# Attention and two expert layers: first-batch products tile by tile on three rotating PSUM banks, and some row sums by squares on ScalarE

## The chip, the core and the metric

The kernel runs on one core of a Trainium2 chip. Its engines run side by side and wait for each other by semaphores: TensorE (PE, its weight loads counted as PEld), VectorE (DVE), ScalarE (ACT), GpSimd (POOL) and SyncE (SP), the last two mostly issuing DMA. The metric is the device time of one execution in microseconds.

## What is computed

Block-causal attention, a gated product layer, and a squared-ReLU layer:

```python
def reference(q, k, v, w1, w2, w3, w_out, w_in, w_out2):   # cut
    scores = q @ k.T / sqrt(64)                # B 4, H 8, S 576, D 64
    scores = where(block_i >= block_j, scores, -1e9)   # blocks of 64
    x = softmax(scores) @ v                    # as 2304 tokens x 512
    a, b = x @ w1, x @ w2                      # 512 -> 1024
    x = ((a * b) @ w3) @ w_out                 # 1024 -> 1024 -> 512
    g = relu(x @ w_in) ** 2                    # 512 -> 2048
    return g @ w_out2                          # 2048 -> 512
```

## The kernel before

The inputs come as raw 64-bit words. A weight tile is converted by two ACT and two DVE instructions (`convert`, L287: ACT L319 and L323, DVE L329 and L332) and then split into a high and a low piece, so that three products of pieces give one accurate product. A w1/w2 tile (`w12_tile(f)`, f from 0 to 7, L380) holds 128 columns of w1 and the same 128 of w2. It needs a scale first: the squared row sums of its two halves (`wsum`; half 0 by an ACT Square with an accumulator, L407, half 1 by a DVE reduction L394 and a tiny square L400) go through a two-column matmul (`norm_scale`, L351) and a few tiny DVE instructions, and then ACT (L278) writes the high piece and DVE (L281) the low one, half by half.

Attention runs in 16 pairs of heads, 4 pairs for each of the 4 batches. A pair has score matmuls (`s`, L757), row maxima on DVE (`nm`, L783 and L791), exponentials on ACT (L816), multiplications by the reciprocal sums (`p`, ACT L857, DVE L864), and the product with v into `pv_bank` (L949). ACT and DVE split that into the pieces of x for the products: `x0h`, `x0l` for token group 0 (320 tokens of the batch), `x1h`, `x1l` for group 1 (256 tokens); DVE's low piece is L965. Pairs 0 to 3 take another way, through transposes `tp` (L900).

`w3 @ w_out` is folded first, row block by row block (`setup_rows(i)`, i from 0 to 7, L1089: products `po`, evictions `w3o` on ACT L1116 and DVE L1121). For each batch `first_block(b, g)` then makes, for group 0 and after it for group 1, the products `ab` of x with all eight w1/w2 tiles (`accumulate`, 12 matmuls for w1 and 12 for w2, emitted in chunks of 6, at L1040), evicts them (`a`: ACT L1166, DVE L1184), splits their product into high and low (`g`: ACT L239, DVE L242) and multiplies by `w3o` (`y`, L1040). After the last batch's x come the normalisations and the second layer (`second_block`).

PSUM holds a pool of five banks for attention and, until all of rows, transposes and scales of the first batch are through, a pool with one `po` bank and two `tp` banks. `begin_blocks` (L1131) closes the latter and opens a pool of three `mm` banks for `ab` and `y`; it is a step that waits for every user of the old pool.

A planner (`Order.emit`, L117) writes each engine's list: an instruction has a key, a cost and the steps it needs, and the planner picks among the ready ones by key and by its own count of time. The key of the n-th conversion comes from `conv_key` (L1854); for the w1/w2 tiles it is

```python
K12 + K12S * (n - 13)      # K12 = 60, K12S = 2
```

`SPARE` is a planner's allowance for the attention steps of pairs 4 and later. Where the planner's own clock has a gap on PE early in the program, `warm_up(gap)` (L520) fills it with 128-wide dummy matmuls, one per 0.11 of the gap. `x_scale_0` (L433) takes the largest absolute v of the first batch's four pairs, by four DVE reductions of 640 elements (L440), for the scale of the first batch's x.

Of the kernel before, what the change touches and what calls it, by code (L numbers as in the profile page):

```python
# [7 lines left out]
F32 = mybir.dt.float32  # L8
# [11 lines left out]
P = 128  # L20
# [3 lines left out]
DM = H * D  # L24
# [146 lines left out]
def fused_kernel(ctx: ExitStack, tc: tile.TileContext, qT, kT, vp, va, w12, w3t, wo, wb, out):  # L171
# [32 lines left out]
    ps0_stack = ExitStack()  # L204
    pools["p0"] = ps0_stack.enter_context(tc.tile_pool(name="ps0", bufs=1, space=PSUM, side="right"))
# [14 lines left out]
    K12 = 60.0  # L220
    K12S = 2.0
# [6 lines left out]
    SPARE = 2.0  # L228
    S_SPARE = 0.7
# [24 lines left out]
    ON_V = (1,)  # L254

# [124 lines left out]
    def w12_tile(f, after):  # L380
# [5 lines left out]
        for half in range(2):  # L386
# [3 lines left out]
            if half in ON_V:  # L390
# [13 lines left out]
            junk = at_buf("junk", 1, [P, 512], BF16, f"junk_{f}_{half}")  # L404
# [3 lines left out]
                    junk(), x(), AF.Square, accum_out=sums()[:, half : half + 1]  # L408
# [23 lines left out]
    def x_scale_0():  # L432
# [3 lines left out]
        for p in range(KDM):  # L436
            v = raws[p][2]
            od.op(
                DVE, c_dve(640),
                lambda v=v, p=p: dve.tensor_reduce(  # L440
                    out=vq()[:, p : p + 1], in_=v().rearrange("p a b c -> p (a b c)"), op=ALU.max, axis=AX.X,
                    apply_absolute_value=True,
                ),
                [(v,)], [(vq, p)], key,
            )
        m = at_buf("vq2", 1, [P, 1], F32, "vq2")
        od.op(
            DVE, c_dve(8), lambda: dve.tensor_reduce(out=m(), in_=vq(), op=ALU.max, axis=AX.X),
            [(vq, p) for p in range(KDM)], [(m,)], key,
        )  # L450
        od.op(
            DVE, c_dve(8), lambda: dve.tensor_tensor(out=m(), in0=m(), in1=m(), op=ALU.mult), [], [(m,)], key
# [41 lines left out]
    def spare(p):  # L494

        return SPARE if p >= KDM else 0.0
# [22 lines left out]
    warm_out = buf("p0", "po", 1, [P, 512], F32, "warm_out")  # L519
# [363 lines left out]
    def transpose(p, g, a, pf, weights, key):  # L883
# [7 lines left out]
        for part, (todo, n) in enumerate(((mains, P), (lasts, 64))):  # L891
            tp = buf("p0", "tp", 2, [P, 512], F32, f"tp_{name}_{part}")
# [151 lines left out]

    class Acc:
# [43 lines left out]
    def setup_rows(i):  # L1089
# [865 lines left out]
```

## Time and profile before

| what | us |
| --- | --- |
| median of 3 runs | 883.93 |
| the runs | 882.22, 883.93, 889.14 |
| profiled execution, its own time | 883.62 |
| its span in the trace | 881.5 |

Between span and time lie 2.1 us that the trace doesn't show. Views of the trace are of this one execution: busy time is the time in which an engine ran something, idle time ahead of a group is put down to whoever released it, and the granted clock is TensorE's as a share of full speed.

### The profile page before, as it was taken

To read this page: it belongs to the slowest core of one execution; us is meant where nothing else is said; L and a number is where in the kernel's file an instruction comes from. 1 tells how busy PE (TensorE), PEld (TensorE's weight loads), DVE (VectorE), ACT (ScalarE), POOL (GpSimd) and SP (SyncE) were. 2 spreads that over 40 slices of the span, in tenths; PEclk is the share of its full clock that TensorE was granted. 3 is DMA by queue.
4 is the path that set the end of the run, shared out by engine and by line. 5 is a ranking of instruction groups with operands and counts; after the bars stand their busy time and mean duration, and the time that the engine had idled before them with its cause. 6 is when DMAs were issued, how large, how long until landed. Compare 5 with 4: busy or idle time off the path is not lost.

```text
span 881.5 us, 18383 instructions
## 1 busy us (share of the span) xinstructions
PE 850.7 (97%) x7143; PEld 643.7 (73%) x7147; DVE 632.6 (72%) x1470; ACT 571.7 (65%) x1304; POOL 107.9 (12%) x202
## 2 busy tenths in 40 slices
PE   7799988899999999999999999999999999999998
PEld 6477875588877888779979877666666666666664
DVE  5987979888778787763993788997853474375443
ACT  5987878677766676774895696664544464464343
POOL 5111112020121101002221111000010000000000
PEclk8999998899999999999999999999999999999999
DMA  8833348589998999883563342000020002001001
GB/s 312 321 123 104 122 147 231 125 149 185 183 196 158 184 167 177 155 136 111 195 204 119 105 143 73 1 25 1 2 97 1 1 29 67 1 1 48 1 1 48
DMA packets 104247, 98.06 MB, mean 111 GB/s; under 512 B 82976, under 2 KB 86816, under 8 KB 102752
## 3 DMA queue, kind: packets, MB, share of 16 engines
q0 software_dynamic: 17568, 69.09, 24.6%
q1 hardware_dynamic: 86592, 27.80, 18.9%
q8 instruction: 56, 0.92, 0.4%
q14 instruction: 31, 0.25, 0.1%
HBM read 60.69 MB, written 9.44 MB: 80 GB/s over the span
## 4 chain that ended last, share of the span: by engine, by line
PE 59%; DVE 3%; ACT 1%; issue 0%; DVEq 0%
PE o L1785 20%; PE p L1721 16%; PE ab L1040 11%; PE y L1040 7%; PE h L1636 2%; PE pv_bank L949 1%; PE s L757 1%; PE ny L1343 0%; DVE s L1663 0%; DVE nm L791 0%; DVE g L271 0%; DVE ob L1795 0%; DVE c L1742 0%; DVE p L864 0%; PE nq L1464 0%
## 5 line engine op out<-in xcount | busy, mean ns | idle before, releaser
L1785 PE MATMUL o<-wb,g 128*128 128x512 f16 x864 | 194.5, 379 | 0.1
L1040 PEld LDWEIGHTS <-w 128*128 128x128 f16 x1536 | 147.8, 99 | 51.8 <-ACT w L278 4.7
L1785 PEld LDWEIGHTS <-g 128*128 128x128 f16 x864 | 84.0, 98 | 92.4 <-issue 0.6
L1040 PE MATMUL ab<-x0h,w 128*128 128x320 f16 x512 | 112.8, 307 | 6.8 <-ACT w L278 3.1
L1040 PE MATMUL y<-g,w3o 128*128 128x320 f32 (+1 forms) x768 | 110.1, 299 | 0.5 <-DVE g L242 0.5
L816 ACT ACTIVATE pf<-s,nm 128x192 f32<-128x192 f32 (+4 forms) x160 | 82.9, 527 | 39.6 <-DVE nm L799 39.5
L1040 PEld LDWEIGHTS y<-g,w3o 128*128 128x128 f32 x768 | 103.6, 188 | 3.8 <-issue 1.9
L1609 ACT ACTIVATE c<-c,beta 128x512 f32<-128x512 f32 x64 | 45.4, 713 | 81.5 <-DVE c L1742 81.4
L1040 PE MATMUL ab<-x1h,w 128*128 128x256 f16 x512 | 87.9, 273 | 0.5 <-DVE a L1184 0.5
L1721 PEld LDWEIGHTS <-wb 128*128 128x128 f16 x768 | 75.2, 98 | 15.8 <-issue 0.2
L271 DVE TENSOR_TENSOR g<-c,g 128x512 f16<-128x512 f32 x64 | 43.7, 689 | 48.8 <-ACT g L269 48.8
L1040 PE MATMUL ab<-x0l,w 128*128 128x320 f16 x256 | 78.4, 306 | 0.0
L864 DVE SCALAR_TENSOR_TENSOR p<-pf,r,p 128x192 f16<-128x192 f32 (+2 forms) x120 | 62.6, 546 | 16.4 <-ACT p L857 15.7
L1040 PE MATMUL ab<-x1l,w 128*128 128x256 f16 x256 | 69.8, 272 | 0.0
L857 ACT ACTIVATE p<-pf,r 128x192 f16<-128x192 f32 (+2 forms) x120 | 60.8, 559 | 5.0 <-ACT pf L816 1.6
L1040 PE MATMUL po<-wo,w 128*128 128x256 f32 (+1 forms) x360 | 55.5, 303 | 8.6 <-DVE w3o L1121 4.8
L1721 PEld LDWEIGHTS <-st 128*128 128x128 f16 x576 | 56.4, 98 | 7.4
L1742 DVE TENSOR_TENSOR c<-p,x 128x512 f32<-128x512 f32 x32 | 22.1, 690 | 50.9 <-PE p L1721 40.2
L1040 PEld LDWEIGHTS po<-wo,w 128*128 128x128 f32 x360 | 47.1, 195 | 14.0 <-DVE w3o L1121 3.9
L757 PE MATMUL s<-kraw,qraw 64*128 64x288 f32 (+4 forms) x384 | 54.5, 409 | 1.2 <-ACT pf L816 1.2
L332 DVE CUSTOM_DVE_ANT_0 cx<-raw,cx 128x1024 uint16<-128x1024 uint16 (+1 forms) x61 | 47.6, 781 | 2.9 <-ACT raw L323 0.4
L319 ACT ACTIVATE raw<-raw 128x512 f32<-128x512 f32 (+1 forms) x61 | 46.4, 763 | 1.6 <-DMA raw<-in_w 1.4
(213 smaller groups left out, 1645.6 us busy)
## 6 DMA issues: line engine op xcount, KB each, us to landing
raw<-in_wb POOLq DMA_DIRECT2D x32, 512.0 KB, 4.9
raw<-in_w3t POOLq DMA_DIRECT2D x8, 1024.0 KB, 12.6
raw<-in_w POOLq DMA_DIRECT2D x16, 512.0 KB, 5.0
vraw<-in_vp POOLq DMA_DIRECT2D x16, 320.0 KB, 4.9
qraw<-in_qT POOLq DMA_DIRECT2D x16, 288.0 KB, 4.1
kraw<-in_kT POOLq DMA_DIRECT2D x32, 144.0 KB, 4.3
yraw<-ydram POOLq DMA_DIRECT2D x8, 512.0 KB, 4.7
vmix<-v SPq DMA_DIRECT2D x24, 160.0 KB, 4.4
```

Of the source, the lines that this page charges most:

```text
L271: DVE, c_dve(n), lambda: dve.tensor_tensor(out=lo(), in0=src(), in1=hi(), op=ALU.subtract), kh + ks, kl, key
L319: act.activation(up, up, AF.Prelu, scale=2.0**-112, alpha=2.0**32)
L332: dve.tensor_tensor(out=x(), in0=x(), in1=words()[1], op=ALU.add)
L757: pe.matmul(o[:, h] if t == 4 else o, q()[rows, q_start(t) : q_start(t) + 128], keys_()[rows, c], start=True, stop=True,)
L816: act.activation(o, view(a, t), AF.Exp, bias=nm()[:, k, a : a + 1], scale=SCALE, accum_out=ssum()[:, k, a : a + 1],)
L857: lambda o=o, nk=nk, a=a, k=k, w=weights, p16=p16, r=r: act.activation(p16()[:, o : o + nk], w(a, k), AF.Copy, scale=r()[:, k, a : a + 1]),
L864: lambda o=o, nk=nk, a=a, k=k, w=weights, p16=p16, r=r: dve.scalar_tensor_tensor(out=p16()[:, o + nk : o + 2 * nk], in0=w(a, k), scalar=r( ...
L1040: pe.matmul(acc(), l, r, start=k == 0, stop=k == len(mms) - 1)
L1609: lambda: act.activation(src(), src(), AF.Relu, scale=beta()[:, j, k : k + 1]),
L1721: pe.matmul(acc()[:, TH * half : TH * half + TH], lhs(a, kc), y[yn]()[:, kc], start=n == 0, stop=n == len(mms) - 1,)
L1742: DVE, c_dve(n), lambda: dve.tensor_tensor(out=o(), in0=x(), in1=y(), op=ALU.add), r, w, K_EVICT
L1785: pe.matmul(o(), g[gx]()[:, cols], wt(f)[:, a, 512:1024], start=(begin and n == 0), stop=(last and n == 2),)
```

## The change

The old `begin_blocks` and its second PSUM pool go. One pool of a `po` bank and two `tp` banks stays for the whole program, and `bank3` hands them out in turn to every accumulation that used `mm`. `first_block` is now called once for a batch: in batch 0 it walks over the w1/w2 tiles, and for each tile does group 0 and then group 1, with the `y` products of both groups after all tiles; in batches 1 to 3 the order of the code is as it was. The pieces `g` of group 1 in batch 0 get a place of their own, the tiles that held the first w_out (`w8_0`, `w8_1`). Rows 6 and 7 of the fold are listed after pair 3, 512 wide in a bank of their own each (24 matmuls instead of 48 of 256). The row sums of the second halves of w1/w2 tiles 5, 6 and 7 are ACT Squares, and so are the four reductions of `x_scale_0`, whose result is now a sum of squares where it was the square of the largest value. The w1/w2 conversions have keys from 50 in steps of 4, the allowance of pairs 4 to 7 is 1.0, and the dummy matmuls after the first gap are counted at 0.062 each: 114 of them become 175 (in stretches of 45, 32, 1, 35, 1 before and 45, 40, 16, 58, 16 after).

```diff
@@ PSUM pools, planner numbers @@
-    pools["p0"] = ps0_stack.enter_context(tc.tile_pool(name="ps0", bufs=1, space=PSUM, side="right"))
+    pools["pm"] = ctx.enter_context(tc.tile_pool(name="psM", bufs=1, space=PSUM, side="right"))
...
-    K12 = 60.0
-    K12S = 2.0
+    K12 = 50.0
+    K12S = 4.0
...
     SPARE = 2.0
+    PO_SPLIT = 6
+    SPARE_1 = 1.0
...
+    SQ_A = 5
@@ w12_tile @@
-            if half in ON_V:
+            if half in ON_V and f < SQ_A:
@@ x_scale_0 @@
             od.op(
-                DVE, c_dve(640),
-                lambda v=v, p=p: dve.tensor_reduce(
-                    out=vq()[:, p : p + 1], in_=v().rearrange("p a b c -> p (a b c)"), op=ALU.max, axis=AX.X,
-                    apply_absolute_value=True,
+                ACT, c_act(640, 0.14),
+                lambda v=v, p=p, junk=junk: act.activation(
+                    junk(), v().rearrange("p a b c -> p (a b c)"), AF.Square, accum_out=vq()[:, p : p + 1]
                 ),
...
-            DVE, c_dve(8), lambda: dve.tensor_reduce(out=m(), in_=vq(), op=ALU.max, axis=AX.X),
+            DVE, c_dve(8), lambda: dve.tensor_reduce(out=m(), in_=vq(), op=ALU.add, axis=AX.X),
@@ warm_up @@
-        for _ in range(int((0.8 * gap - 0.2) / 0.11)):
+        n = int((0.8 * gap - 0.2) / warm_cost[0])
+        if n > 0:
+            warm_cost[0] = 0.062
+        for _ in range(n):
@@ Acc and its banks @@
+    def bank3(name):
+
+        n_bank3[0] += 1
+        tag, n = ("po", 1) if n_bank3[0] % 3 == 0 else ("tp", 2)
+        return buf("pm", tag, n, [P, 512], F32, name)
...
-        def __init__(self, n, name, pool_="pm", tag="mm", bufs=3, full=512):
-            self.b = buf(pool_, tag, bufs, [P, full], F32, name)
+        def __init__(self, n, name, *home):
+            self.b = buf(*home, [P, 512], F32, name) if home else bank3(name)
@@ setup_rows @@
-        for half in range(2) if i else (None,):
+        for half in range(2) if 0 < i < PO_SPLIT else (None,):
...
+            if i < PO_SPLIT:
+                acc = Half(po_bank[0], cols, range(2) if half is None else (half,))
+            else:
+                acc = Acc(DM, f"po_{i}")
@@ first_block; ab_products holds the old loop's body for one f and one group @@
-    def begin_blocks():
-
-        begin = od.op("N", 0.0, open_blocks)
...
+    def first_block(b):
+        gs = [Products() for _ in GS]
+        if b:
+            for g in range(2):
+                for f in range(KFF):
+                    ab_products(b, g, f, gs[g])
+                y_products(b, g, gs[g])
+            return
+        for f in range(KFF):
+            for g in range(2):
+                ab_products(b, g, f, gs[g])
+        for g in range(2):
+            y_products(b, g, gs[g])
@@ g_at: where the pieces of the products of group 1, batch 0, lie @@
+            if b or not g:
+                gs.tiles.append(g_buf(f // 4, name))
+            else:
+                gs.tiles.append(buf("base", f"w8_{f // 4}", 1, [P, 8 * gn], F32R, name))
@@ the program @@
-        setup_rows(i)
+        if i < PO_SPLIT:
+            setup_rows(i)
...
+            for i in range(PO_SPLIT, KFF):
+                setup_rows(i)
...
-            begin_blocks()
...
-        for g in range(2):
-            first_block(b, g)
+        first_block(b)
```

PE's list where the first batch's products begin, before. A name `ab_0_1_0_0` is batch 0, group 1, tile 0, w1 (a last 1 is w2); what follows is a buffer's number.

```order
L1040 MATMUL ab_0_0_0_0_1625<-x0h0_0_468,w12_0_1224 128x320
...
L1040 MATMUL ab_0_0_0_1_1650<-x0h0_0_468,w12_0_1224 128x320
...
L1040 MATMUL ab_0_0_1_0_1674<-x0h0_0_468,w12_0_1224 128x320
...
L1040 MATMUL ab_0_0_7_1_2156<-x0h0_0_468,w12_3_1995 128x320
...
L1040 MATMUL y_0_0_0_2089<-g_0_0_0_1695,w3o_1_731 128x320 x6
...
L1040 MATMUL ab_0_1_0_0_2471<-x1h0_0_524,w12_0_1224 128x256
```

The same place after:

```order
L1044 MATMUL po_6_1475<-wo_0_314,w3_6_1272 128x512 x6
...
L1044 MATMUL po_7_1569<-wo_0_314,w3_7_1482 128x512 x6
...
L1044 MATMUL ab_0_0_0_0_1657<-x0h0_0_532,w12_0_1254 128x320
...
L1044 MATMUL ab_0_1_0_0_1703<-x1h0_0_588,w12_0_1254 128x256
...
L1044 MATMUL ab_0_1_0_1_1726<-x1h0_0_588,w12_0_1254 128x256
...
L1044 MATMUL ab_0_0_1_0_1747<-x0h0_0_532,w12_0_1254 128x320
```

All sixteen products of group 0 and its first `y` stood ahead of group 1's; now tile 0 serves both groups before tile 1 comes, with rows 6 and 7 just ahead.

DVE's list around the split of the last w1/w2 tile, `w12_3` from `cx_28` and `cx_29`, before. `a_0_0_6` is the eviction of tile 6, `p16_4_2` and `nm_5_0` are softmax steps of pairs 4 and 5, `wsc` is the tile's scale.

```order
L1184 SCALAR_TENSOR_TENSOR a_0_0_6_2041<-ab_0_0_6_1_2029,ab_back_0_1203,a_0_0_6_2041 128x320
L357 TENSOR_SCALAR nh_14_2070<-pv_bank_256 128x2
L259 TENSOR_SCALAR wsc_7_2072<-nh_14_2070 128x2
L259 TENSOR_SCALAR w12_back_1201<-nh_14_2070 128x2
L425 TENSOR_SCALAR ab_back_0_1203<-w12_back_1201,isx_0_270 128x2
L864 SCALAR_TENSOR_TENSOR p16_4_2_0_2054<-pf_4_2_0_2025,r_4_2_2050,p16_4_2_0_2054 128x576
L242 TENSOR_TENSOR g_0_0_4_1941<-a_0_0_6_2041,g_0_0_4_1941 128x320
L281 SCALAR_TENSOR_TENSOR w12_3_1995<-cx_28_1959,wsc_7_2072,w12_3_1995 128x512
L281 SCALAR_TENSOR_TENSOR w12_3_1995<-cx_29_2023,wsc_7_2072,w12_3_1995 128x512
L864 SCALAR_TENSOR_TENSOR p16_4_2_1_2062<-pf_4_2_1_2036,r_4_2_2050,p16_4_2_1_2062 128x576
L774 MEMSET s_5_0_2064 64x2x2x64
L791 TENSOR_REDUCE nm_5_0_2111<-s_5_0_2064 128x2 x2
```

After, from the eviction of group 1's tile 5 on:

```order
L1192 SCALAR_TENSOR_TENSOR a_0_1_5_2257<-ab_0_1_5_1_2250,ab_back_0_1242,a_0_1_5_2257 128x256
...
L243 TENSOR_TENSOR g_0_1_4_2203<-a_0_1_5_2257,g_0_1_4_2203 128x256
L868 SCALAR_TENSOR_TENSOR p16_5_1_0_2278<-pf_5_1_0_2227,r_5_1_2268,p16_5_1_0_2278 128x448
...
L787 TENSOR_REDUCE nm_5_2_2338<-s_5_2_0_2283 128x1
...
L969 SCALAR_TENSOR_TENSOR x0l0_1_2366<-pv_bank_289,vback_1_1845,x0h0_1_2350 128x320
...
L261 TENSOR_SCALAR wsc_7_2454<-nh_14_2388 128x2
...
L283 SCALAR_TENSOR_TENSOR w12_3_2177<-cx_28_2179,wsc_7_2454,w12_3_2177 128x512
L283 SCALAR_TENSOR_TENSOR w12_3_2177<-cx_29_2352,wsc_7_2454,w12_3_2177 128x512
```

Behind the split there were pair 4's last multiplication and pair 5's first maxima; now pair 5's multiplications and last maxima, six evictions of group 1 and pair 4's `x0l0_1` stand ahead of it.

PE's list where batch 1 begins, before. Pair 7 is the last whose x batch 1's products need: `x0h3_1`, `x0l3_1`, from `pv_bank` after `pt_7_0`.

```order
L949 MATMUL pv_bank_256<-pt_7_0_0_2981,v16_7_2765 64x256
...
L1040 MATMUL y_0_1_3_3289<-g_0_1_0_2552,w3o_1_731 128x256 x6
...
L757 MATMUL s_8_2_0_3351<-kraw_8_2649,qraw_8_2640 128x288
...
L1040 MATMUL y_0_1_3_3289<-g_0_1_4_2896,w3o_3_1472 128x256 x6
...
L1040 MATMUL ab_1_0_0_0_3379<-x0h0_1_2168,w12_0_1224 128x320
...
L949 MATMUL pv_bank_256<-pt_7_1_0_3119,v16_7_2765 64x128
...
L1040 MATMUL ab_1_0_0_0_3379<-x0h3_1_3338,w12_0_1224 128x320
...
L1040 MATMUL ab_1_0_0_0_3379<-x0l3_1_3349,w12_0_1224 128x320
```

After:

```order
L1044 MATMUL y_0_1_3_3278<-g_0_1_4_2203,w3o_3_1579 128x256 x6
...
L1044 MATMUL ab_1_0_0_0_3320<-x0h0_1_2350,w12_0_1254 128x320
...
L1044 MATMUL ab_1_0_0_1_3331<-x0h0_1_2350,w12_0_1254 128x320
...
L761 MATMUL s_8_2_0_3340<-kraw_8_2748,qraw_8_2742 128x288
...
L953 MATMUL pv_bank_289<-pt_7_0_0_3052,v16_7_2844 64x256
...
L1044 MATMUL ab_1_0_0_0_3320<-x0h2_1_3055,w12_0_1254 128x320
...
L1044 MATMUL ab_1_0_0_0_3320<-x0h3_1_3388,w12_0_1254 128x320
...
L1044 MATMUL ab_1_0_0_0_3320<-x0l3_1_3393,w12_0_1254 128x320
```

Between pair 7's first product with v and the `x0h3_1` that comes from it there were `y` products, scores, nine products of older x and pair 7's second part; now three products on `x2` stand there.

## Rows read from the trace of the kernel before

**Rows 1.** The page, part 1: busy time and share of PE over the span.
```profile
PE 850.7 (97%) x7143; PEld 643.7 (73%) x7147; DVE 632.6 (72%) x1470; ACT 571.7 (65%) x1304; POOL 107.9 (12%) x202
```

**Rows 2.** Windows: busy us of PE, PEld, DVE, ACT, POOL, then clock, DMA.
```profile
0.00:101.00 101.00, 88.05 (x719) 71.25 (x719) 81.51 (x182) 81.28 (x183) 24.09 (x49) 0.95 0.56 199
101.00:171.20 70.20, 59.01 (x428) 43.49 (x428) 61.55 (x165) 53.39 (x122) 11.28 (x21) 0.93 0.59 168
171.20:241.50 70.30, 69.82 (x776) 60.67 (x776) 57.91 (x156) 50.86 (x150) 10.85 (x20) 1.00 0.94 172
116.30:170.40 54.10, 43.23 (x280) 30.16 (x278) 46.14 (x128) 41.86 (x94) 8.07 (x15) 0.91 0.60 168
170.40:242.90 72.50, 72.02 (x791) 62.21 (x790) 60.11 (x161) 51.70 (x152) 11.25 (x21) 1.00 0.94 172
242.90:881.50 638.60, 632.42 (x5217) 467.32 (x5218) 430.23 (x967) 385.36 (x848) 61.28 (x112) 1.00 0.35 84
```

**Rows 3.** Groups by shape, PE, 116.32 to 170.44: count, busy, mean ns, idle before.
```profile
L1040 PE MATMUL ab<-x0h,w 128*128 128x320 f16 x112 | 27.6, 335 | 6.8 <-ACT w L278 3.1 <-DVE w L281 2.7 <-DVE w3o L1121 1.0
...
L1040 PE MATMUL po<-wo,w 128*128 128x256 f32 x72 | 10.0, 289 | 3.0 <-ACT w3o L1116 1.8 <-DVE w3o L1121 1.2
```

**Rows 4.** Time line, PE: start us, us, engine, line, operation, tiles, count.
```profile
167.47 2.05 PE L757 MATMUL s<-kraw,qraw 64*128 64x192 f32 x16
169.45 1.15 PE L1040 MATMUL y<-g,w3o 128*128 128x320 f32 x6
...
172.17 0.52 PE L949 MATMUL pv_bank<-pt,v 128*64 128x256 f16 x8
...
173.24 0.31 PE L1040 MATMUL ab<-x0h,w 128*128 128x320 f16 x1
...
181.14 0.97 PE L949 MATMUL pv_bank<-pt,v 128*64 128x128 f16 x28
...
183.05 1.24 PE L757 MATMUL s<-kraw,qraw 64*128 64x288 f32 x8
...
211.55 0.38 PE L1040 MATMUL ab<-x1h,w 128*128 128x256 f16 x2
...
211.88 0.38 PE L1040 MATMUL ab<-x1h,w 128*128 128x256 f16 x2
```

**Rows 5.** Groups by shape, DVE, 0 to 260 us.
```profile
L791 DVE TENSOR_REDUCE nm<-s 128x2 f32<-128x896 f32 x10 | 10.9, 1088 | 0.3
...
L864 DVE SCALAR_TENSOR_TENSOR p<-pf,r,p 128x448 f16<-128x448 f32 x10 | 6.8, 682 | 2.4 <-ACT p L857 2.4
...
L394 DVE TENSOR_REDUCE wsum<-cx 128x1 f32<-128x512 f32 x8 | 5.4, 681 | 0.1
...
L1184 DVE SCALAR_TENSOR_TENSOR a<-ab,ab_back,a 128x256 f32<-128x256 f32 x8 | 3.8, 476 | 0.4 <-PE ab L1040 0.3
...
L242 DVE TENSOR_TENSOR g<-a,g 128x256 fp32r<-128x256 f32 x8 | 3.3, 419 | 0.0
...
L440 DVE TENSOR_REDUCE vq<-vraw 128x1 f32<-128x640 f32 x4 | 3.2, 806 | 0.0
```

**Rows 6.** Time line, DVE: two short instructions, and the last w1/w2 tile's split.
```profile
165.75 0.16 DVE L400 TENSOR_TENSOR wsum<-wsum 128x1 f32<-128x1 f32 x1
165.82 0.16 DVE L829 TENSOR_SCALAR r<-ssum 128x2 f32<-128x2 f32 x1
...
169.83 1.41 DVE L281 SCALAR_TENSOR_TENSOR w<-cx,wsc,w 128x512 f16<-128x512 f32 x2
```

**Rows 7.** Groups by shape, ACT, 0 to 260 us.
```profile
L407 ACT ACTIVATE junk<-cx 128x512 bf16<-128x512 f32 x8 | 5.0, 626 | 3.2 <-DVE cx L332 3.2
```

**Rows 8.** Time line, PE, at the first products of batch 1.
```profile
242.94 0.30 PE L1040 MATMUL ab<-x0l,w 128*128 128x320 f16 x1
```

**Rows 9.** Time line, DVE, there.
```profile
241.45 0.55 DVE L965 SCALAR_TENSOR_TENSOR x0l<-pv_bank,vback,x0h 128x320 f16<-128x320 f32 x1
```

**Rows 10.** Time line, PE, the fourth stretch of dummy matmuls.
```profile
15.95 3.69 PE L523 MATMUL warm_out<-warm 128*128 128x128 bf16 x35
```

More of the change, by code (lines that the diff above doesn't have):

```diff
@@ L403, in w12_tile @@
                 continue
-            junk = at_buf("junk", 1, [P, 512], BF16, f"junk_{f}_{half}")
+            junk = at_buf("junk", 1, [P, 640], BF16, f"junk_{f}_{half}")
             od.op(
@@ L407, in w12_tile @@
                 lambda x=x, half=half, junk=junk: act.activation(
-                    junk(), x(), AF.Square, accum_out=sums()[:, half : half + 1]
+                    junk()[:, :512], x(), AF.Square, accum_out=sums()[:, half : half + 1]
                 ),
@@ L494, in spare @@
     def spare(p):
[L496 removed]
+        return 0.0 if p < KDM else SPARE_1 if p < 2 * KDM else SPARE
     raws = {}
@@ new lines, in fused_kernel, with g_at @@
+    last_y = []
+    def g_at(b, g, f, gs):
+        gn = GS[g][1]
+        wide = GMAX if b or not g else gn
+        m = f % 4
+        if not m:
+            name = f"g_{b}_{g}_{f}"
+            if b or not g:
+                gs.tiles.append(g_buf(f // 4, name))
+            else:
+                gs.tiles.append(buf("base", f"w8_{f // 4}", 1, [P, 8 * gn], F32R, name))
+        t = gs.tiles[f // 4]
+        return (
+            lambda: t()[:, 2 * m * wide : 2 * m * wide + gn],
+            lambda: t()[:, (2 * m + 1) * wide : (2 * m + 1) * wide + gn],
+            (t, "h", m), (t, "l", m),
+        )
@@ new lines, in fused_kernel, with __init__, ab_products @@
+    class Products(list):
+        def __init__(self):
+            self.tiles = []
+    def ab_products(b, g, f, gs):
+        gn = GS[g][1]
+        x = xs[b, g]
+        av = buf("mo1", "a", 2, [P, GMAX], F32, f"a_{b}_{g}_{f}")
+        for which in range(2):
+            acc = Acc(gn, f"ab_{b}_{g}_{f}_{which}")
+            mms = []
+            for kc in range(KDM):
+                for a, xn in PRODS:
+                    o = which * 512 + kc * P
+                    mms.append((
+                        lambda a=a, xn=xn, o=o, kc=kc: (w12_view(f, a)[:, o : o + P], x[xn][kc]()),
+                        [w12_key(f, a, which), (x[xn][kc],)],
+                    ))
+            accumulate(acc, mms, gn, next_key(), c_mm16)
+            back = Part(ab_back[b], 2 * f + which, 1)
+            if which == 0:
+                od.op(
+                    ACT, c_act(gn, 0.09),
+                    lambda acc=acc, back=back: act.activation(av()[:, :gn], acc(), AF.Copy, scale=back()),
+                    [acc.key, (ab_back[b], f)], [(av,)], K_EVICT,
+                )
+                continue
+            hi, lo, kh, kl = g_at(b, g, f, gs)
+            od.op(
+                DVE, c_dve(gn, 0.06),
+                lambda acc=acc, back=back: dve.scalar_tensor_tensor(
+                    out=av()[:, :gn], in0=acc(), scalar=back(), in1=av()[:, :gn], op0=ALU.mult, op1=ALU.mult
+                ),
+                [acc.key, (ab_back[b], f)], [(av,)], K_EVICT,
+            )
+            split(hi, lo, lambda: av()[:, :gn], gn, ([kh], [kl], (av,)), K_EVICT)
+            gs.append(((hi, lo), (kh, kl)))
```

74 lines of the change are left out of this document (10 added, 64 removed).

## The prediction

> **What bounds the kernel now.** I read the page's busy shares first: TensorE (PE) is busy 850.7 us, 97% of the span of 881.5 [rows 1]. So nearly all of the time is PE's own work, and this change takes no product away except by making some wider. It can only win where PE is idle or runs at less than the full clock, and only if nothing new makes it wait. The windows tell where that is. From 242.9 us to the end PE is busy 632.42 of 638.60 us at full clock, and from 170.4 to 242.9 it is busy 72.02 of 72.50. From 116.3 to 170.4, the stretch of group 0's products in batch 0, it is busy only 43.23 of 54.10, and the granted clock is 0.91 [rows 2]. Here lie 54.10 - 43.23 = 10.9 us of idle time. The shortfall of the clock is worth about 0.09 * 54.1 = 4.9 us more: an estimate, since it takes the mean clock as a loss on the whole stretch. Together some 15.8 us can be had. The rest of the idle time before 116 us is the start of the program, which the change touches only lightly.
>
> What PE waits for in that stretch the groups by shape say: 6.8 of the idle us are ahead of `ab<-x0h`, released by ACT's split of the w1/w2 tile (3.1), DVE's (2.7) and, once, the end of the old PSUM pool, shown as `w3o` (1.0); 3.0 are ahead of the fold's products `po` [rows 3]. So PE is fed one w1/w2 tile at a time, uses each for 24 products of 320, and waits for the next. The tiles come from ACT and DVE. In 101.0 to 171.2, which begins where tile 0's DVE split ends and ends just where tile 7's does (169.83 + 1.41 us [rows 6]), DVE is busy 61.55 of 70.20 us, 88%, and ACT 53.39, 76% [rows 2]. DVE is the nearest to its limit.
>
> **The change, part by part.** *Order of the products.* Each tile now feeds group 1 as well. A product of 256 takes 0.11 us from one to the next (three from 211.55 to 211.88 [rows 4]), so group 1 adds 24 * 0.109 = 2.6 us of PE work for each tile, with x that is long there. Of group 1's eight tiles seven come ahead of tile 7's first product: 7 * 2.6 = 18.3 us. PE's order also puts pair 4's products with v there, 1.1 us (172.17 to 173.24) and 1.9 us (181.14 to 183.05), and scores of 2.05 and 1.24 us, and moves six `y` products behind (1.15 us, 0.9 without the overlap with what follows) [rows 4]. That is 18.3 + 3.0 + 3.3 - 0.9 = 23.7 us of work which PE did after 170.4 and can now do while it would wait. If it never waited, it would reach tile 7 at 116.3 + (54.1 - 15.8) + 23.7 = 178.3 us, and the 15.8 us would all be gained.
>
> *When tile 7 is ready.* DVE's list up to that split loses four reductions of 806 ns and three row sums of 681 ns with their tiny squares (0.16 us), and gains six evictions and six splits of group 1 (476 and 419 ns), the softmax of pair 5 up to its third part, and pair 4's `x0l` (0.55 us [rows 9]). Two records that follow each other overlap by some 0.08 us (165.75 + 0.16 against 165.82 [rows 6]), so I take 0.08 off each. Then: -4 * 0.73 = -2.9; -3 * (0.60 + 0.07) = -2.0; rows 6 and 7 in two evictions of 512 instead of four of 256, -0.2; 6 * (0.39 + 0.34) = +4.4; pair 5 and the end of pair 4, six reductions (the largest 1088 ns) for 3.7, nine multiplications (the middle shape 682 ns [rows 5]) for 4.1 and eleven tiny ones for 1.5, +9.3; `x0l`, +0.5. The sum is +9.1 us. If DVE takes it all into its idle 8.65 us, the split ends at about 171.6. At its share of 88% it ends at 171.2 + 9.1 / 0.88 = 181.5. The middle, 176.5, is just short of PE's arrival at 178.3. So the two engines meet, and I take 2.5 us of waiting at the tiles instead of 10.9: 1 us as the middle of 0 to 3.2 at tile 7, the rest at earlier tiles, whose gate is the same chain. The conversions' keys from 50 in steps of 4 only help to spread this chain; by the order it still goes in the tiles' sequence, so I give them no price.
>
> *Row sums on ACT.* ACT's Square of 512 takes 626 ns [rows 7], DVE's reduction 681 [rows 5]; ACT has 16.8 us idle in 101.0 to 171.2. It takes over seven such instructions, three of them here, some 2 us, and it has room. So the sum goes by 2.0 us off DVE for as much on ACT. The Trainium skill speaks against this part: "ScalarE: Activation LUTs", section Rules for kernel authors, gives additions and multiplications to VectorE, up to about three times as fast for an element in bf16. By that, an estimate, DVE would be relieved of only a third of ACT's 626 ns, 0.6 us in the three, and the split would end 1.4 us later; for these f32 halves the two rows stand against it, 681 ns to 626.
>
> *The handover to batch 1.* From 170.4 PE had 72.5 us to batch 1's first products; 23.7 of it has moved ahead, so 48.8 are left. With 2.5 us of waiting it gets there at 178.3 + 2.5 + 48.8 = 229.6. DVE had 57.91 us of work in 171.2 to 241.5 [rows 2], of which pair 5, six units of group 1 and `x0l`, 14.2 us, have moved ahead: 43.7 are left, 43.7 us at full use or 43.7 / 0.824 = 53.1 at the old share. From 171.6 to 181.5 that gives 215 to 235, with 225 in the middle. Before, pair 7's low piece was done at 241.45 + 0.55 = 242.0 [rows 9], close ahead of the products of batch 1 (242.94 [rows 8]), with `y` products, scores and older pieces lying between pair 7's first product with v and the products that read it. Now three products stand there, 0.4 us, while ACT's high and DVE's low piece follow one another at about half a us each. So at least 0.7 us of waiting is new, and up to 235 - 229.6 = 5.4 us if DVE is late. I take 2.
>
> *The rest.* The barrier of the old pool is the 1.0 us in [rows 3] and is counted. Three rotating banks are as many as before, so no eviction is nearer to PE than it was; `po` as third bank costs nothing once the rows are through. Rows 6 and 7: 96 products of 256 at 10.0 / 72 = 0.139 us [rows 3] are 13.3 us. As 48 products of 512 they take 13.3 too if time goes with the columns, and 6.7 at the least, if a product costs as much as one of half its width; I take 12.8, a gain of 0.5, near the first, since 256 is the only width of this kind that the stretch shows. The early stretch: up to 101 us ACT is busy 81.28 us and DVE 81.51 [rows 2]. ACT gets four Squares of 640, some 3 us by the 626 ns of 512, and DVE loses as much; what waits for that scale is the first x alone. The dummy matmuls fill idle time; the fourth stretch, 35 of them in 3.69 us [rows 10], becomes 58. I take -0.2 for all of this, within -1.5 and +3. Batches 2 and 3 and the second layer keep their order; DVE has 33% idle there (430.23 busy of 638.60), so what is won by 230 us is kept.
>
> *Sum*, against the profiled execution's 883.62 us, which is 0.3 under the median of 883.93: -15.8 + 2.5 + 2 - 0.5 - 0.2 = -12.0, **871.6 us**.
>
> **The rivals.** *All of it is gained.* DVE works at full use, as it can once more is ready for it: no waiting, -15.8 - 0.5 - 1.5 gives 866. Against it speaks the handover.
>
> *DVE takes PE's place as the bound.* Up to 241.5 us DVE is busy 81.51 + 61.55 + 57.91 = 201 us [rows 2], so 40.5 idle. Up to pair 7's last x it now has about 4.9 us less, 196. If it idles as much as before, since it also waits for ACT, scores and DMA, batch 1 starts 4.9 us earlier and no more: 879. That is within 1% of before, and the likeliest of the cases other than mine.
>
> *The same chain, slower.* The change puts more softmax and eviction between the tiles, each waiting for PE or ACT in turn, so that DVE's list, which is fixed, stops more often before it reaches a split and then pair 7's low piece. The point is DVE's busy share until the handover: 196 / 241.5 = 0.81 is even, before it was 201 / 241.5 = 0.83. At 0.78 the handover is at 251 and the time is 893, slower by 1%. Against it: PE waits less for each tile, so evictions are ready sooner.
>
> *Early loss.* If the fourth stretch of dummies doesn't end before the scores it stands ahead of, 58 of them take 58 * 3.69 / 35 = 6.1 us, 2.4 more than now, all on PE's path; then 874.
>
> *It doesn't do what it says.* If tiles still arrive one by one with PE waiting for each, as where the split of the next tile is queued behind group 1's evictions on DVE, PE only trades idle time for group 1's work and the gain is that of the barrier and the wide rows, 1.5 us: 882.
>
> **How the numbers follow.** A change of 1% is about what a measurement of this kernel can tell from none: below 875.1 is faster, above 892.8 slower. My forecast has 0.45, the full gain 0.12, the early loss 0.08 (mostly still faster); DVE as bound 0.20, no effect 0.10, slower 0.05. The predicted time is the forecast's. The first three lie at 866 to 877 with the bounds of their terms, one in thirty of them above 875.1; DVE as bound is at 874 to 882 and gives a little to faster. That makes faster 0.64, same 0.31, slower 0.05. The range for 8 in 10 goes from 864, the full gain with the products of 512 at their best half, to 881, which leaves out the no-effect and the slower case.
>
> **What would show it.** In the changed profile PE should be busy over 95% of the stretch from about 115 to 180 us, with the granted clock near 1; the waits ahead of `ab<-x0h` released by `w` should shrink from 6.8 us to about 2; `ab` of group 1 should lie between the tiles. The last split on DVE should end near 177 to 181 and batch 1's products should start near 230, with one wait of 1 to 3 us ahead of them, released by `x0h` or `x0l`. I am wrong if DVE's idle time up to there is still 40 us, if PE's idle time moves from the tiles to the handover, or if the scores behind the fourth stretch of dummies, now at 15.95 + 3.69 us, come more than a us later.

## The result and the profile after

The changed kernel takes 875.75 us (median of 16 runs; 883.94 for the kernel before, 16 runs). The ratio is 0.9904, with a 95% interval of 0.9883 to 0.9925. Its profiled execution has a span of 872.8 us, 8.7 us under the one of before. The forecast was 871.6, so the sign and the range were right and about two thirds of the gain came. The time lies just above the prediction's own line for faster (875.1): in its terms the outcome is the one that it gave 0.31, not the one that it gave 0.64.

The page, part 1, of the changed kernel, against [rows 1]:

```profile
PE 849.3 (97%) x7160; PEld 641.9 (74%) x7160; DVE 626.9 (72%) x1457; ACT 575.5 (66%) x1316; POOL 107.6 (12%) x202
```

PE's busy time has hardly changed; what went is idle time. The windows of the changed kernel over the tiles' stretch and over the handover, in columns as in [rows 2]:

```profile
116.00:186.00 70.00, 66.30 (x578) 50.50 (x577) 65.84 (x175) 61.87 (x152) 11.34 (x21) 1.00 0.70 174
186.00:250.00 64.00, 63.58 (x674) 53.26 (x672) 51.38 (x138) 45.57 (x139) 11.94 (x22) 1.00 1.03 190
```

The same windows of the kernel before:

```profile
116.00:186.00 70.00, 59.13 (x464) 43.99 (x461) 60.53 (x163) 52.54 (x128) 10.70 (x20) 0.93 0.63 160
186.00:250.00 64.00, 63.52 (x715) 53.73 (x714) 50.51 (x137) 46.16 (x131) 12.02 (x23) 1.00 1.01 189
```

In the first window PE's idle time fell from 10.9 us to 3.7 and the granted clock is full where it was 0.93. DVE is now busy 65.84 of 70 us: within this window it works through the idle time that it had. In the second window nothing is worse. In these two windows that is the picture that was forecast.

Where the 8.7 us came from can be read between places that both programs pass: the products `po` of the fold behind a wait of 0.47 us, at 61.22 (before) and 61.88 (after), from here on the fold's wait, and the start of the second layer's first product, at 505.9 and 497.2. The kernel before, in pieces:

```profile
0.00:61.22 61.22, 49.23 (x371) 39.46 (x371) 48.78 (x99) 47.84 (x95) 17.59 (x37) 0.92 0.75 272
61.22:116.30 55.08, 53.80 (x490) 44.54 (x490) 47.34 (x119) 44.97 (x117) 9.71 (x18) 1.00 0.34 108
242.90:505.90 263.00, 261.23 (x2671) 218.22 (x2669) 192.25 (x486) 185.46 (x466) 44.04 (x83) 1.00 0.71 159
505.90:881.50 375.60, 371.20 (x2548) 249.10 (x2550) 237.99 (x482) 199.90 (x384) 17.24 (x29) 1.00 0.09 32
```

The kernel after:

```profile
0.00:61.88 61.88, 51.30 (x432) 42.00 (x432) 46.13 (x94) 50.92 (x103) 17.20 (x37) 0.94 0.74 269
61.88:115.50 53.62, 51.24 (x438) 41.23 (x439) 44.83 (x115) 43.00 (x112) 9.06 (x17) 1.00 0.34 106
115.50:180.14 64.64, 60.94 (x533) 46.63 (x532) 61.42 (x165) 58.01 (x143) 10.46 (x21) 1.00 0.68 173
180.14:234.76 54.62, 54.20 (x557) 46.30 (x556) 44.47 (x119) 37.00 (x110) 11.31 (x21) 1.00 1.00 197
234.76:497.20 262.44, 260.25 (x2654) 216.83 (x2654) 191.97 (x487) 186.77 (x469) 42.28 (x79) 1.00 0.71 159
497.20:872.80 375.60, 371.41 (x2552) 248.88 (x2550) 238.04 (x482) 199.83 (x384) 17.24 (x29) 1.00 0.10 32
```

From the second layer on both take 375.60 us. Up to the fold's wait the changed kernel is 0.66 us later, for a reason that the paragraph on the clock below gives. In between it gains 9.36 us: 5.7 of idle time (1.28 + 10.87 + 0.48 + 1.77 [rows 2, and the fence on before] against 2.38 + 3.70 + 0.42 + 2.19) and 3.65 of busy time, from the clock and the wide rows.

The waits that are left at the tiles, time line of PE in the changed kernel:

```profile
136.94 0.18 PE L353 MATMUL pv_bank<-wsum,ones 128*128 128x2 bf16 x1 [0.34 <-DVE wsum L402]
...
140.33 0.49 PE L609 MATMUL pv_bank<-vdiag,ones 128*128 128x128 f32 x2 [0.24 <-DVE vdiag L603]
...
148.50 0.17 PE L353 MATMUL pv_bank<-wsum,ones 128*128 128x2 bf16 x1 [1.02 <-ACT junk L409]
...
156.49 0.16 PE L353 MATMUL pv_bank<-wsum,ones 128*128 128x2 bf16 x1 [0.61 <-ACT junk L409]
...
176.80 0.16 PE L353 MATMUL pv_bank<-wsum,ones 128*128 128x2 bf16 x1 [1.43 <-ACT junk L409]
```

They no longer stand ahead of `ab<-x0h`, but ahead of the little matmul that makes a tile's scale, because behind it PE has group 1's products of the tile in hand. The last one, 1.43 us, is put down to ACT's Square. ACT and DVE there:

```profile
176.03 0.63 ACT L409 ACTIVATE junk<-cx 128x512 bf16<-128x512 f32 x1 [0.56 <-DVE cx L334]
```

```profile
172.26 1.67 DVE L868 SCALAR_TENSOR_TENSOR p<-pf,r,p 128x448 f16<-128x448 f32 x4
...
175.31 0.69 DVE L334 CUSTOM_DVE_ANT_0 cx<-raw,cx 128x1024 uint16<-128x1024 uint16 x1
...
178.73 1.41 DVE L283 SCALAR_TENSOR_TENSOR w<-cx,wsc,w 128x512 f16<-128x512 f32 x2
```

ACT stood idle 0.56 us ahead of that Square until DVE's conversion of the same half (175.31 + 0.69) was through, and that conversion stands in DVE's list behind pair 5's multiplications (172.26, four in 1.67 us) and maxima. So the wait points at the order of DVE's list: in e4 and e12 below, where that conversion stands earlier, the last wait ahead of a scale is 0.48 and 0.68 us. The last split ends at 178.73 + 1.41 = 180.1, within the 171.6 to 181.5 of the forecast.

### The profile page after: what moved, and what is told of

Its sections match the earlier page's. It is cut to its first block, busy times and chain, and to the rows that moved or that the text cites. A ratio compares the mean times of both kernels' runs of the same rounds, so it can differ in the third digit from the quotient of the medians.

```text
span 872.8 us, 18419 instructions
## 1 busy us (share of the span) xinstructions
PE 849.3 (97%) x7160; PEld 641.9 (74%) x7160; DVE 626.9 (72%) x1457; ACT 575.5 (66%) x1316; POOL 107.6 (12%) x202
## 4 chain that ended last, share of the span: by engine, by line
PE 44%; DVE 7%; ACT 3%; issue 1%; DMA 1%; POOL 0%; DVEq 0%; POOLq 0%
PE o L1810 20%; PE p L1746 16%; PE y L1044 4%; PE ab L1044 3%; DVE cx L334 1%; DVE wb L283 1%; PE h L1661 1%; DMA raw<-in_wb 1%; DVE cx L331 1%; ACT wb L280 1%; DVE rm L1517 1%; DVE s L1688 0%; DVE a L1192 0%; PE ny L1368 0%; DVE g L243 0%
## 5 line engine op out<-in xcount | busy, mean ns | idle before, releaser
L1044 PE MATMUL ab<-x0h,w 128*128 128x320 f16 x512 | 109.5, 300 | 0.1
L1044 PE MATMUL ab<-x0l,w 128*128 128x320 f16 x256 | 76.6, 299 | 0.3 <-DVE x0l L969 0.3
L1192 DVE SCALAR_TENSOR_TENSOR a<-ab,ab_back,a 128x320 f32<-128x320 f32 (+1 forms) x64 | 32.6, 510 | 20.3 <-PE ab L1044 19.7
## 6 DMA issues: line engine op xcount, KB each, us to landing
raw<-in_w3t POOLq DMA_DIRECT2D x8, 1024.0 KB, 13.3
```

What stands on the lines that cost most here:

```text
L1044: pe.matmul(acc(), l, r, start=k == 0, stop=k == len(mms) - 1)
L1192: lambda acc=acc, back=back: dve.scalar_tensor_tensor(out=av()[:, :gn], in0=acc(), scalar=back(), in1=av()[:, :gn], op0=ALU.mult, op1=ALU.mult
```

## The experiments

Each time was taken beside that of the kernel before, so ratios are compared rather than medians; the changed kernel's is 0.9904. Theory A is that of the forecast: the gain is group 1's products where PE waited for the next tile. Its first rival, B, has the gain in DVE's relief and the earlier keys; the others (C to L) stand where they come up.

**The order undone (e1).** Batch 0 goes group by group again; the rest stays as changed.

```diff
-        for f in range(KFF):
-            for g in range(2):
-                ab_products(b, g, f, gs[g])
-        for g in range(2):
-            y_products(b, g, gs[g])
+        for g in range(2):
+            for f in range(KFF):
+                ab_products(b, g, f, gs[g])
+            y_products(b, g, gs[g])
```

> The changed kernel with batch 0's products again group by group (all eight tiles for group 0, then y, then group 1); everything else as changed. Theory A (the gain is group 1's products standing where PE waited for the next tile): the waits of PE ahead of ab and of the scale's matmul come back to 8 to 11 us, the half clock comes back, time 880 to 885, 5 to 9 us over the changed kernel. Rival B (the gain is DVE's relief and the earlier conversion keys, the order of the products is neutral): 874 to 878, waits at the tiles under 5 us.

891.88 us, ratio 1.0075 [1.0045, 1.0105]. The windows:

```profile
116.00:186.00 70.00, 56.65 (x435) 38.81 (x434) 62.60 (x168) 57.42 (x143) 10.77 (x20) 0.93 0.72 164
186.00:250.00 64.00, 62.46 (x698) 54.14 (x697) 50.49 (x134) 44.10 (x125) 11.36 (x21) 1.00 1.13 203
```

The waits are back (13.4 us) and the clock is 0.93 again, so B falls. But the time is 7 us above before, which A did not say: without the order, the rest of the change costs time.

**The order alone (e8) and the banks alone (e9).** e8 sets everything else back; e9 sets the order back too.

```diff
-    K12 = 50.0
-    K12S = 4.0
+    K12 = 60.0
+    K12S = 2.0
-    PO_SPLIT = 6
-    SPARE_1 = 1.0
+    PO_SPLIT = 8
+    SPARE_1 = 2.0
-    SQ_A = 5
+    SQ_A = 8
-            warm_cost[0] = 0.062
+            warm_cost[0] = 0.11
...
```

> Only the order tile by tile in batch 0 with the three rotating banks (group 1's pieces in their own place, no barrier); row sums, scale of x, keys, rows 6 and 7, allowance and dummies as before. Theory A (the order is the gain): 874 to 878, at least three quarters of the changed kernel's gain, waits at the tiles of 3 to 6 us. Rival B (squares, keys and moved rows are needed to feed it): 879 to 884, waits at the tiles of 7 us or more.

> Only the three rotating banks without the barrier and the place for group 1's pieces; group by group and all else as before. Theory A: the barrier is worth the 1.0 us that the trace of before shows at the first product of group 0, so -2 to +1 us against before, 882 to 885. Rival G (the new banks tie the products to each other or to the rows and make PE wait, which is why the kernel with the groups' order restored was 7 us slower than before): +3 to +7 us, 887 to 891.

e8: 886.62 us, ratio 1.0024 [1.0007, 1.0042]. e9: 886.51, ratio 1.0029 [1.0011, 1.0047]. The banks without the barrier cost some 2.5 us, between what A and G said. The barrier's wait is gone in e9, but PE then waits the longer for the split tiles, 9.4 us from 116 to 171 us where it was 6.8 with the barrier's 1.0 in [rows 3]:

```profile
L1047 PE MATMUL ab<-x0h,w 128*128 128x320 f16 x122 | 30.0, 335 | 9.4 <-DVE w L283 4.9 <-ACT w L280 4.6
```

And the order alone gains nothing: A's time is missed by 9 us. But its waits at the tiles are gone, as A said, and B's 7 us are not there. The windows of e8 show where it went:

```profile
116.00:186.00 70.00, 65.38 (x592) 52.16 (x594) 62.20 (x169) 55.34 (x136) 8.61 (x16) 1.00 0.65 155
186.00:250.00 64.00, 56.01 (x532) 45.63 (x530) 47.16 (x129) 41.99 (x122) 13.54 (x25) 0.92 0.96 186
```

4.6 us idle at the tiles, at full clock, and then 8.0 us idle at the handover with the clock at 0.92. What had been won was given back to batch 1's start, clock and all. PE there in e8:

```profile
230.94 2.05 PE L764 MATMUL s<-kraw,qraw 64*128 64x192 f32 x16
236.82 1.32 PE L764 MATMUL s<-kraw,qraw 64*128 64x288 f32 x2 [3.82 <-DVE p L871]
240.07 2.28 PE L764 MATMUL s<-kraw,qraw 64*128 64x288 f32 x6 [1.93 <-ACT pf L823]
```

Pair 8's first scores (16 in 2.05 us) end at 233.0, and the next instruction in PE's list is pair 8's last scores, which wait 3.82 us and then 1.93 more, the second time for ACT's exponentials `pf`. The profile puts the first wait down to DVE's `p`, which ended as ACT's first exponentials of pair 8 did; ACT had stood for pair 8's maxima before it could begin them:

```profile
234.83 0.42 ACT L823 ACTIVATE pf<-s,nm 128x192 f32<-128x192 f32 x1 [2.19 <-DVE nm L806]
```

The same two steps of pair 8 in the kernel before, with 10.0 us of other products between them, and then in the changed kernel:

```profile
228.72 2.05 PE L757 MATMUL s<-kraw,qraw 64*128 64x192 f32 x16
...
240.79 1.24 PE L757 MATMUL s<-kraw,qraw 64*128 64x288 f32 x8
```

```profile
220.94 2.05 PE L761 MATMUL s<-kraw,qraw 64*128 64x192 f32 x16
...
231.22 1.24 PE L761 MATMUL s<-kraw,qraw 64*128 64x288 f32 x8
...
234.76 0.30 PE L1044 MATMUL ab<-x0l,w 128*128 128x320 f16 x1 [0.29 <-DVE x0l L969]
```

In the changed kernel 8.2 us of `y` and `ab` products lie between them (222.99 to 231.22), and there is no wait at the scores in either. DVE is busy only 47.16 of 64 us in e8's window: this is not DVE at its limit but the way from scores to maxima to exponentials, with too little for PE to do beside it.

**What puts work there: squares (e10), allowance (e11), keys (e4), allowance undone (e7).** e10 is e8 with `SQ_A = 5`, e11 is e8 with `SPARE_1 = 1.0`; the other two are the changed kernel with

```diff
-    K12 = 50.0
-    K12S = 4.0
+    K12 = 60.0
+    K12S = 2.0
```

in e4, and in e7 with

```diff
-    SPARE_1 = 1.0
+    SPARE_1 = 2.0
```

Theory I, formed on e8's rows, is that the handover waits when too few `y` products are left behind pair 7's last scores.

> Order tile by tile with the rotating banks, and the row sums of tiles 5 to 7 by squares on ACT; keys, rows, allowance, dummies and scale of x as before. Pair 7's last scores stand in y product 2, with some 4.5 us of y products left. Theory I: waits at the handover of 2.5 to 4 us (order alone: 7.5), time 879 to 883. Rival K (the 2 us of DVE work taken off are the gain, wherever the lists put things): waits there as with the order alone less 2, 5.5 us, 884 or above.

> Order tile by tile with the rotating banks, and the allowance of 1.0 for pairs 4 to 7; all else as before. Pair 7's last scores stand in y product 3, with some 3 us of y products left. Theory I: waits at the handover of 4 to 5 us, time 881 to 885. Rival J (the allowance alone is enough): waits under 1.5 us, 876 to 879.

> Conversion keys of the w1/w2 tiles again from 60 in steps of 2; the last tile's split then stands 24 rows earlier in DVE's list. Theory A: the last wait ahead of the scale's matmul (1.43 us) goes, since the conversion is no longer behind pair 5's softmax, but tiles in the middle may be waited for; time -2 to +2 us, 873 to 878. Rival F (the spread keys are what lets DVE keep up): waits at the tiles of 6 us or more, 879 or above.

> The changed kernel with the allowance of pairs 4 to 7 back at 2.0. In PE's list pair 7's last scores then stand in y product 1 of group 1 (of 0 to 3) instead of 0, some 7 us of y products ahead of batch 1 instead of 10. Theory I (the handover waits only when fewer y products than about 7 to 8 us are left behind pair 7's last scores): waits there 0 to 1.5 us, time 875 to 878. Rival J (the allowance itself is what carries the gain into batch 1): 5 us or more at the handover, 881 or above.

e10: 879.45 us, 0.9928 [0.9900, 0.9955], waits from 186 to 250 of 3.9 us: as theory I said. e11: 889.39, 1.0042 [1.0018, 1.0067], waits of 6.5 us: over what I said, and J falls. e4: 879.02, 0.9920 [0.9889, 0.9951], waits at the tiles down to 2.4 us and at the handover up to 4.5. e7: 878.89, 0.9908 [0.9875, 0.9940], the time about the changed kernel's, but in the profiled execution (span 881.7) 5.6 us idle from 186 to 250, where I had said 0 to 1.5. So theory I, as I had put it (`y` products behind pair 7's last scores), is not the measure: e7 has more of them than e10 and waits longer. In e10 the two score steps of pair 8 are

```profile
227.34 2.05 PE L764 MATMUL s<-kraw,qraw 64*128 64x192 f32 x16
...
233.28 0.75 PE L764 MATMUL s<-kraw,qraw 64*128 64x288 f32 x2 [0.53 <-ACT pf L823]
235.78 2.08 PE L764 MATMUL s<-kraw,qraw 64*128 64x288 f32 x6 [1.75 <-ACT pf L823]
```

3.4 us of other products lie between them (229.39 to 232.75), and 2.3 us of waits follow. These rows fall in line by another measure: 0 us of work between pair 8's first and last scores and 5.75 us of waits ahead of the latter in e8; 0.9 and 4.0 in e11; 0.9 and 4.4 in e4; 3.4 and 2.3 in e10; 8.2, none, in the changed kernel. Work and waits add up to 4.9 to 5.75 us in the four that wait: an estimate of what the way from the first scores to the last ones takes. I formed the measure after these runs. The other kernels, which were not used for it, bear it out: e5, e2, e12, e3, e6, e9, the kernel before and e1 have 6.8 to 13.7 us of work there and no wait at pair 8's last scores. In e4, whose last scores wait twice:

```profile
231.19 0.75 PE L761 MATMUL s<-kraw,qraw 64*128 64x288 f32 x2 [2.69 <-DVE p L868]
233.65 2.28 PE L761 MATMUL s<-kraw,qraw 64*128 64x288 f32 x6 [1.71 <-ACT pf L820]
```

e7 has 5.6 us of work between the two steps and waits for other things, one of them in between:

```profile
233.99 0.30 PE L1044 MATMUL ab<-x0h,w 128*128 128x320 f16 x1 [2.13 <-ACT ys L1235]
...
242.16 0.42 PE L1044 MATMUL ab<-x0l,w 128*128 128x320 f16 x1 [2.38 <-DVE x0l L969]
```

ACT's `ys`, and the `x0h` that `x0l` needs, stand in ACT's list behind multiplications for pairs 7 and 8, and these stood waiting for the DMA that reads the buffer which they write (`pt<-p`).

```profile
228.37 0.78 ACT L861 ACTIVATE p<-pf,r 128x576 f16<-128x576 f32 x1 [2.05 <-DMA pt<-p]
...
237.53 0.91 ACT L861 ACTIVATE p<-pf,r 128x192 f16<-128x192 f32 x2 [3.29 <-DMA pt<-p]
```

Whether that is in each of its runs one profile can't say; they lie between 876.2 and 883.5.

**Keys from 56 in steps of 3 (e12), and from 50 in steps of 3 (e6).**

```diff
-    K12 = 50.0
-    K12S = 4.0
+    K12 = 56.0
+    K12S = 3.0
```

> The changed kernel with conversion keys from 56 in steps of 3: the last tile's split stands 15 rows earlier in DVE's list, ahead of pair 5's last maxima, and pair 7's last scores stay in y product 0, 10 us ahead of batch 1. Theory I with A: waits at the tiles of 1 to 2.5 us (3.4 in the changed kernel from 120 us on), none of over 1 us at the handover, time 872.5 to 875. Rival L (what is won at the tiles comes back at the handover, since DVE's work up to there is the same): waits at the handover grow by as much, time 875 to 877.

> Conversion keys from 50 in steps of 3 instead of 4; the last tile's split stands 21 rows earlier in DVE's list, and the conversion of tile 7 ahead of pair 5's last softmax steps. Theory A (the 3.7 us left ahead of the scale's matmul come from DVE's list order): waits of 0.5 to 2.5 us, time 872.5 to 875. Rival C (the Square on ACT or DVE's sum of work sets it): waits stay at 3 us or more, 875 to 878.

e12: 873.43 us, ratio 0.9855 [0.9826, 0.9885], the fastest of all; its interval just touches the changed kernel's. Its windows, and pair 8's two score steps:

```profile
116.00:186.00 70.00, 67.45 (x583) 51.34 (x582) 66.03 (x179) 61.52 (x151) 11.78 (x22) 1.00 0.71 174
186.00:250.00 64.00, 62.36 (x656) 52.66 (x654) 49.97 (x130) 44.20 (x128) 11.98 (x23) 0.97 1.01 190
```

```profile
225.43 2.05 PE L761 MATMUL s<-kraw,qraw 64*128 64x192 f32 x16
...
235.34 1.24 PE L761 MATMUL s<-kraw,qraw 64*128 64x288 f32 x8
```

2.55 us idle at the tiles, 1.64 from 186 to 250, which is a wait for `x1l` at 203.9, none at the scores, with 7.9 us of work between them. L's time is missed, but of the waits it is right in this execution: what was won at the tiles (1.15 us) is given back at 203.9. What e12 gains lies elsewhere. Its span, 872.2, is only 0.6 us under the changed kernel's because this execution reaches the fold's wait at 62.94, 1.06 us later; from there to the second layer it takes 433.70 us against 435.36. These 1.7 us are about what this wait of the changed kernel in batch 2 costs:

```profile
384.94 0.41 PE L1044 MATMUL y<-g,w3o 128*128 128x320 f32 x1 [1.53 <-ACT g L240]
```

e3 has it too (1.54 us); e12 has no wait over 0.3 us from 250 us to the second layer. Why the keys of batch 0's conversions take it away was not followed up. e6: 877.95 us, 0.9934 [0.9911, 0.9957]: a miss. Its waits at the tiles from 130 us on are 2.5 us, as A said, but with those keys the products of tile 0 start before rows 6 and 7 and PE waits at 108 to 113 us for `w3o` (1.50), the Square (1.99) and `pf` (0.56), with the clock at 0.83 from 100 to 120.

**Row sums back on DVE (e2), fewer dummies (e3), rows in their old place (e5).** `SQ_A = 8`; the second line of `warm_cost` back to 0.11; `PO_SPLIT = 8`.

> Row sums of tiles 5 to 7, second half, back on DVE (reduction and tiny square), x_scale_0 still on ACT. Theory A (the waits left ahead of the scale's matmul, 3.1 us behind ACT's Square, are set by DVE's list, where the conversion of the last tile stands behind pair 5's softmax): the waits stay at 2.5 to 5 us and end on DVE's reduction instead, time 0 to +2 us against the changed kernel, 875 to 878. Rival C (the Square on ACT is what the scale waits for): the waits fall under 1.5 us and the time to 872 to 874.

> Dummy matmuls counted as before (118 instead of 175), nothing else; the lists are otherwise the same. Theory A (the dummies fill idle time and raise the clock early, but their lead of 0.95 us at pair 0's scores is gone again by 62 us): the half clock comes back at 12 to 20 us, pair 0's scores start near 19.5, and the time is within 1 us of the changed kernel, 875 to 877. Rival D (early time is on the path to the end): +1 to +2 us, 877 to 878. Rival E (more dummies only cost): -1 us or more.

> Rows 6 and 7 in the old place and 256 wide again, the rest as changed. Theory A (the move of the rows is neutral: it frees 0.6 us of products and brings 1.1 us of waits between 94 and 106): within 2 us of the changed kernel, 874 to 877.5. Rival H (the rows' move is what gives DVE its room before the first tile): waits at the tiles grow by 3 us or more, 879 or above.

e2: 877.27 us, 0.9913 [0.9881, 0.9946], same as the changed kernel; waits at the scales of 2.7 us (3.4 in the changed kernel), now ended by DVE's `wsum` at tiles 6 and 7 (0.47 and 0.87), so there the Square was not what the scale waits for (the wait of 1.02 us before them stays, released by an ACT Square as in the changed kernel), and 2.1 us at the handover, ahead of `ab`. e3: 875.32, 0.9891 [0.9863, 0.9920], the same too; pair 0's scores came at 17.6 us, earlier than with more dummies, where I had said 19.5. The extra dummies gain nothing. e5: 877.69, 0.9930 [0.9907, 0.9953], 2 us over the changed kernel, just past what A allowed. H falls: the waits at the tiles are 3.0 us, no more than the changed kernel's 3.6. The old rows bring eight waits between 114 and 134 us, in pairs like these:

```profile
115.29 0.97 PE L1044 MATMUL po<-wo,w 128*128 128x256 f32 x6 [0.47 <-ACT w3o L1131]
116.85 0.98 PE L1044 MATMUL po<-wo,w 128*128 128x256 f32 x6 [0.59 <-DVE w3o L1136]
```

In place of 256 wide halves in one bank that PE, ACT and DVE pass round, the 512 wide rows in banks of their own leave PE busy all of 113 to 133 us.

## Why the prediction came out as it did

*Bound and place.* Right: the gain is idle time and clock between 116 and 180 us, and from the second layer on nothing changed.

*Group 1's products as cover.* Right, and e1 shows it: the same kernel without them idles 13.4 us there. Left at the tiles are 3.7 us where I took 2.5. What I said of DVE was half right:

```profile
101.00:180.14 79.14, 75.11 (x639) 57.26 (x638) 74.74 (x202) 69.32 (x170) 15.16 (x29) 1.00 0.66 174
```

From 101 us to the last split DVE has 13.2 us more to do than before (74.74 against 61.55 [rows 2]). 4.3 of them went into its idle time (8.65 to 4.40), and the rest moved the split from 171.2 to 180.1, near the end of what I had given rather than at its middle of 176.5. Ahead of 101 us its idle time grew by 3.9, so up to the first product on pair 7's `x0l` (234.76) DVE idles 37.9 us: close to the 40 that I had named as a sign of being wrong. It did no harm, since PE had group 1's products in hand and came to tile 7 only at 183.66, behind its split.

*The clock.* Over-sized. I took 4.9 us from the mean clock, and 0.5 from the wide rows; both together gave 3.65 of busy time between the common places. The wide rows gave more than I took: as 48 products of 512 they take 12.0 us, where I had 13.3 for them before.

```profile
L1044 PE MATMUL po<-wo,w 128*128 128x512 f32 x48 | 12.0, 403 | 0.0
```

That leaves some 2.3 us for the clock. And ahead of the common places this execution of the changed kernel loses 0.66 us, where I had a gain of 0.2: after the wait of 2.65 us ahead of the fold's second row, for the first row's `w3o`, PE runs at half clock longer than before, and 28 products take 6.15 us.

```profile
44.03 0.77 PE L1044 MATMUL po<-wo,w 128*128 128x256 f32 x2 [2.65 <-DVE w3o L1136]
45.08 6.15 PE L1044 MATMUL po<-wo,w 128*128 128x256 f32 x28 [0.27 <-DVE w L243]
```

The change does not decide this. e1, e4 and e6 have the same products in the same order on PE up to there, dummies included, and their 28 products take 5.10, 5.05 and 4.76 us, while in e10, whose list on PE begins as in the kernel before, they take 6.32. In e1:

```profile
45.25 5.10 PE L1044 MATMUL po<-wo,w 128*128 128x256 f32 x28 [0.57 <-DVE w L243]
```

These three reach the fold's wait at 61.01, 60.51 and 60.65 us, ahead of the kernel before (61.22). So the early part of a profile can be off by a microsecond whatever the kernel, and one profile each does not tell what the change does to it.

*The step that failed* is the one on the handover with the one on the keys. I took 2 us of new waiting there, with DVE's share of busy time as the price, and gave the conversions' keys "no price". The handover waits only 0.3 us, but not for the reason that I had: the order alone pays 8 us there (e8), and where the lists put pair 8's scores decides whether it is paid. The keys do that in the changed kernel (e4), the squares next to the order alone (e10); for the moved rows no run shows it, and with the squares (e2) or the rows (e5) put back there is still no wait at the scores. The rival *DVE takes PE's place as the bound* is what happens in e8, e11 and e4, by another mechanism than I put: not DVE's share (47 of 64 us busy in e8) but the way from scores to exponentials behind a PE that has run out of other work. Since in the whole change that does not occur, the forecast held, and in part by luck: the handover came out 2.1 us better than I had it, which set off part of the 5.4 us by which the other terms together came out worse; had I been asked of the order alone, I would have forecast a gain that is not there.

*The banks.* I counted the barrier's 1.0 us as gained and three rotating banks as free. By themselves they cost 2.5 us (e9); what they are worth in the whole change no run shows.

*Smaller terms.* The rows' neighbourhood (61 to 116 us) has 1.1 us of new waits, which I had at nought; they come with the keys that I gave no price, since e4, with the keys of before, idles 1.3 us from 61 to 116 where the changed kernel idles 2.9. Batches 1 to 3 have 0.4 more. In all: -7.2 for idle time at the tiles, -3.65 for clock and wide rows, -0.1 at the handover, +1.1, +0.7 and +0.4 make -8.7; I had -8.4, -5.4, +2, 0, -0.2 and 0.

*Row sums on ACT.* e2 says that they are worth nothing measurable in the changed kernel (0.9913 to 0.9904), so neither the 2 us that I gave DVE by the rows nor the 0.6 by the estimate from the Trainium skill ("ScalarE: Activation LUTs", Rules for kernel authors) can be told from it. The Square itself takes 0.63 us in the row above, as in [rows 7]; each is followed by a read of its sum, 0.19 us on ACT, which I left out. Next to the order alone three squares are worth some 8 us by the ratios (e10 against e8), 4.1 of it less idle time from 186 to 250 us, by where the lists then put pair 8's scores.

What stays open: which part of the rest of the change costs 4 us without the order (e1 against e9). From the fold's wait to the second layer e1 takes 451.42 us and e9 447.52, and 3.7 of these 3.9 us are waits of PE: 1.1 from 61 to 116 us, 1.2 at the tiles (13.35 to 12.16) and 1.3 from 186 to 250. No run takes the parts out one by one with the groups in their old order.

## What to carry to other kernels

Work that covers a wait ahead of one boundary is gone from the next: before counting the gain, follow the list on to the next point where all must meet, and look what lies between two steps there that need each other's answer. A planner's keys, costs and allowances that seem to change nothing by themselves can decide that; test the main edit without them and them without it. An engine's busy share does not say that it has time to spare in a chain of short steps over three engines.

## What the runs showed of the hardware

A gap of PE of 2.65 us at 41 to 44 us, ahead of the same products, is followed by a stretch at half clock (1.2 GHz) that is not equally long in every execution: 3.4 us in the kernel before, e1, e4 and e6, 6.8 us in the changed kernel and e10. The granted clock from 44 to 50 us is 0.72 in the kernel before and 0.50 in the changed one. And in e7 ACT stood 2.05 and 3.29 us for DMAs that fetch `pt` from `p`; from 205 to 250 us it waits for them at most 1.8 us in any other kernel here, and not at all in the changed one.
